# Chunk-selected attention and an ELU MLP on one NeuronCore: half-batch blocks in an order that the kernel's own list scheduler writes

## The chip, the cores and the metric

The kernel runs on one core of one Trainium2 chip. The core has five engines with a queue each, and every queue is worked off strictly in order: PE (TensorE: matrix products and transposes), ACT (ScalarE), DVE (VectorE), POOL (GpSimd) and SP (SyncE, which here only issues transfers). Engines wait for each other through semaphores. Products land in PSUM, which has eight banks of 512 float32 columns by 128 partitions. The metric is the device time of one execution in microseconds (us).

## The reference, cut to what matters

Four batches, eight heads, 768 positions, head width 64, all float32. Keys are cut into 24 chunks of 32. For each query and chunk an upper bound of the score is formed from the chunk's smallest and largest key values; each query keeps the six best causal chunks; softmax attention runs over those; the result, as 3072 tokens by 512, goes through a two-layer MLP with ELU between.

```python
ub = np.sum(np.maximum(q[:, :, :, None, :] * k_min[:, :, None, :, :], q[:, :, :, None, :] * k_max[:, :, None, :, :]), axis=-1)
causal = pos[:, None] // chunk >= np.arange(nc)[None, :]
ub = np.where(causal, ub, -1000000000.0)
top_chunks = np.argsort(ub, axis=-1)[..., -top_k:]
scores = scale * np.matmul(q, k.transpose(0, 1, 3, 2))
...
mask = sel & (pos[:, None] >= pos[None, :])
scores = np.where(mask, scores, -1000000000.0)
scores = scores - np.max(scores, axis=-1, keepdims=True)
attn = np.exp(scores)
attn = attn / (np.sum(attn, axis=-1, keepdims=True) + 1e-09)
return np.matmul(attn, v).astype(np.float32)
...
h = x @ w_in                      # 3072 x 512 @ 512 x 2048
g = np.where(h > 0.0, h, alpha * (np.exp(np.minimum(h, 0.0)) - 1.0))
return (g @ w_out).astype(np.float32)
```

## The kernel before

Heads go in pairs, 16 pairs in all, two pairs to a group. For each pair there are three stages, and for each half batch of 384 tokens there is the MLP.

- `prep` (L162): K and Q of the pair, all 768 positions, are transposed on PE in float32, three 128x128 transposes to a PSUM tile (`psK` L169, `psQ` L189). DVE takes the smallest and largest value of each chunk from the K tile (L172, L173); ACT copies the same tile as bf16 into `lhsA` and `lhsB` (L175, L176); POOL lays minimum and range into `kst` (L180, L181). ACT copies the Q tile to float32 (`QTf`) and twice to bf16 (`rhsA`, `rhsB`), and DVE clips `QTf` at zero (`Qrl`, L197). POOL casts V (`cast_v`, L118).
- `select` (L200): for a group of two pairs PE forms the bounds `ub` (L207), DVE transposes them (L210), finds the eight largest per query block (`MAX8`, L215), compares (L217) and transposes back (L221); SP sends the mask into the free rows of `rhsA` and `rhsB` (L224, L225), so that the score product adds it by itself.
- `attend` (L233): scores on PE (L250), exponential on ACT (L253, L256), the causal triangle on DVE (L262, L268), products with V on PE (L280, called PV here), normalising on DVE (L284, L286), transposing back on PE (L291) and copying to `xt` on DVE (L292).
- `mlp` (L295): sixteen first products of four matmuls (L302); each is followed by the exponential on ACT (L306), minus one on POOL (L308) and the join on DVE (L310) into `gT`; then three output tiles of sixteen matmuls (L315).

PSUM is dealt out in fixed shares: two banks for transposes and bounds, two for scores, one for PV, three for the MLP (L69 to L72). The program text runs groups in the order of L345 to L359: attention of two groups makes a batch, and the MLP of that batch is written two groups later, the last MLP at the end. The tile framework reorders the instructions of each engine by itself around that text. The weights are loaded by POOL, each load behind the cast of pair 2 to 5 (L327).

Two rules of the framework matter here. An instruction that reads or overwrites a tile waits for the instruction that last wrote or read it on another engine. And two engines that read the same PSUM bank are kept apart too, in the order in which the program gives the instructions.

Of the kernel before, what the change touches and what calls it, by code (L numbers as in the profile page):

```python
# [15 lines left out]
B = 4  # L16
H = 8
# [9 lines left out]
NQT = S // P  # L27
# [4 lines left out]
BIG = 3.0e38  # L32

NPAIR = H // 2
NSET = 4
Q0 = TOPK * CHUNK
NQB = NCH - TOPK
NQS = S - Q0
HB = NQB // 2
HQ = HB * CHUNK  # L40


@with_exitstack
def kernel(
# [29 lines left out]
    npairs = B * NPAIR  # L74


    def load(t):
        b, r = divmod(t, NPAIR)
        k_pair = ldpool.tile([P, NQT, 2, D], F32, name="k_pair")
        q_pair = ldpool.tile([P, NQT, 2, D], F32, name="q_pair")  # L80
        for h in range(2):
            nc.sync.dma_start(out=k_pair[:, :, h, :],
                              in_=k[b, 2 * r + h].rearrange("(n p) d -> p n d", p=P))
        for h in range(2):
            nc.sync.dma_start(out=q_pair[:, :, h, :],
                              in_=q[b, 2 * r + h].rearrange("(n p) d -> p n d", p=P))
        return k_pair, q_pair

    def load_v(t):
        b, r = divmod(t, NPAIR)  # L90
        v_pair = ldpool.tile([P, NQT, 2, D], F32, name="v_pair")
        for h in range(2):
            nc.sync.dma_start(out=v_pair[:, :, h, :],
                              in_=v[b, 2 * r + h].rearrange("(n p) d -> p n d", p=P))
        return v_pair

    lds = {t: load(t) for t in range(2)}
    ldv = {t: load_v(t) for t in range(2)}


    ident_f = const.tile([P, P], F32, name="ident_f")
    nc.gpsimd.memset(ident_f, 0.0)
    nc.gpsimd.affine_select(out=ident_f, in_=ident_f, compare_op=AOT.not_equal,
                            fill=1.0, base=0, pattern=[[-1, P]], channel_multiplier=1)
    ident_b = const.tile([P, P], BF16, name="ident_b")
    nc.vector.tensor_copy(out=ident_b, in_=ident_f)

    vexts, lhsA, lhsB, rhsA, rhsB, kst = [], [], [], [], [], []
    for s in range(NSET):
        vexts.append(const.tile([P, NQT, 2, D + 1], BF16, name=f"vext{s}"))  # L110
        lhsA.append(const.tile([P, S], BF16, name=f"lhsA{s}"))
        lhsB.append(const.tile([P, S], BF16, name=f"lhsB{s}"))
        rhsA.append(const.tile([P, S], BF16, name=f"rhsA{s}"))
        rhsB.append(const.tile([P, S], BF16, name=f"rhsB{s}"))
        kst.append(const.tile([P, 2, 64], F32, name=f"kst{s}"))

    def cast_v(t):
        return nc.gpsimd.tensor_scalar(out=vexts[t % NSET][:, :, :, 0:D], in0=ldv.pop(t), scalar1=1.0,  # L118
                                       scalar2=0.0, op0=AOT.mult, op1=AOT.add)

    for s in range(NSET):
        nc.vector.memset(kst[s], 0.0)
        nc.vector.memset(vexts[s][:, :, :, D:D + 1], 1.0)
        nc.vector.memset(rhsA[s][64:P, :], 0.0)
        nc.vector.memset(rhsB[s][0:64, :], 0.0)

    econst = const.tile([P, NCH, CHUNK], BF16, name="econst")
    nc.vector.memset(econst, MASKNEG)
    for r0 in (0, 64):
        nc.gpsimd.affine_select(out=econst[r0:r0 + 64], in_=econst[r0:r0 + 64],  # L130
                                compare_op=AOT.is_equal, fill=0.0, base=0,
                                pattern=[[1, NCH], [0, CHUNK]], channel_multiplier=-1)
    for s in range(NSET):
        nc.vector.tensor_copy(out=lhsA[s][64:P, :],
                              in_=econst[64:P].rearrange("p c w -> p (c w)"))
        nc.vector.tensor_copy(out=lhsB[s][0:64, :],
                              in_=econst[0:64].rearrange("p c w -> p (c w)"))

    tri01 = const.tile([P, P], BF16, name="tri01")
    nc.gpsimd.memset(tri01, 1.0)  # L140
    nc.gpsimd.affine_select(out=tri01, in_=tri01, compare_op=AOT.is_ge,
                            fill=0.0, base=0, pattern=[[1, P]], channel_multiplier=-1)
    selb = [const.tile([P, NQB, CHUNK], BF16, name=f"selb{i}") for i in range(2)]
    for i in range(2):
        nc.gpsimd.memset(selb[i], 0.0)

    w_in_sb = const.tile([P, NKK, DFF], BF16, name="w_in_sb")
# [200 lines left out]
    for g in range(ng):  # L348
        attend(2 * g)
        if g + 1 < ng:  # L350
            select(g + 1)
# [38 lines left out]
```

## Time and profile before

| | us |
|---|---|
| three runs, median (lowest to highest) | 381.0 (379.08 to 381.08) |
| the profiled execution, first to last instruction (its span) | 378.3 |
| PE busy | 318.7 |
| ACT busy | 225.4 |
| DVE busy | 205.3 |
| POOL busy | 103.3 |

The median of the runs is 2.7 us above the span of the profiled execution. Busy time counts each matmul from its start to its modelled end, and neighbours overlap, so the PE figure is no measure of how fast PE works; the rows below give starts as well. In the rows of the timeline a start in us comes first, then the duration, the engine, the source line, the operation, `output<-input`, the shape and a count; brackets at the end give the idle time before and who ended it.

### The profile page before, as it was taken

How to read it: one execution, taken by the hardware profiler on the slowest of the kernel's cores; microseconds unless marked ns; L12 is line 12 of the kernel's file. 1: busy time of each engine (PE TensorE's matmuls, PEld its weight loads, DVE VectorE, ACT ScalarE, POOL GpSimd, SP SyncE). 2: the span in 40 equal slices, each digit the busy share in tenths (PEclk: the TensorE clock that was granted, in tenths of full speed). 3: DMA queues.
4: the chain of work that ended last, by engine and by line, in shares of the span. 5: the costliest groups of instructions: out<-in, count | busy, mean ns of one | idle time of the engine just before them, and what ended most of it. 6: DMA issues, size and time to landing. Idle time of an engine off the chain costs nothing.

```text
span 378.3 us, 6504 instructions
## 1 busy us (share of the span) xinstructions
PE 318.7 (84%) x2260; PEld 176.6 (47%) x2272; DVE 205.3 (54%) x594; ACT 225.4 (60%) x489; POOL 103.3 (27%) x228
## 2 busy tenths in 40 slices
PE   1476876889599999599997799999999989979886
PEld 1333444455265455354564454545556444444442
DVE  7553275367477475561694683651867154261540
ACT  1638757858968965950879758653797052350430
POOL 4414022003133112340331231430123053250430
PEclk9995697589989999989998999999999999999999
DMA  9949999935914526501000000102000100101002
GB/s 205 277 74 192 203 181 177 280 71 118 209 42 98 125 71 161 117 2 55 30 12 2 1 14 28 58 0 83 5 11 2 57 29 26 58 3 55 28 2 83
DMA packets 84129, 30.67 MB, mean 81 GB/s; under 512 B 76160, under 2 KB 81024, under 8 KB 84096
## 3 DMA queue, kind: packets, MB, share of 16 engines
q1 hardware_dynamic: 79872, 26.06, 27.7%
q0 software_dynamic: 4224, 4.19, 7.1%
q8 instruction: 18, 0.29, 0.3%
q14 instruction: 15, 0.12, 0.1%
HBM read 27.26 MB, written 6.29 MB: 89 GB/s over the span
## 4 chain that ended last, share of the span: by engine, by line
PE 27%; issue 23%; ACT 21%; POOL 12%; DVE 11%; DMA 4%; POOLq 0%; SPq 0%; ACTq 0%; DVEq 0%
POOL m_sb L308 12%; PE o_ps L315 8%; ACT pt L253 6%; PE sps L250 4%; PE ub L207 4%; PE h_ps L302 4%; DMA k_pair<-in_k_dram 2%; DVE gT L310 2%; PE psQ L189 2%; ACT e_sb L306 2%; ACT QTf L194 1%; PE psK L169 1%; DMA rhsA_137<-selT 1%; ACT pt L256 1%; PE pxt L291 1%
## 5 line engine op out<-in xcount | busy, mean ns | idle before, releaser
L302 PE MATMUL h_ps<-xt,w_in_sb 128*128 128x384 bf16 x512 | 108.4, 333 | 13.2 <-DVE gT L310 12.8
L308 POOL TENSOR_SCALAR m_sb<-e_sb 128x384 f32<-128x384 f32 x128 | 65.9, 518 | 179.0 <-ACT e_sb L306 162.3
L253 ACT ACTIVATE pt<-sps 128x384 bf16<-128x384 f32 (+1 forms) x160 | 80.1, 536 | 37.2 <-PE sps L250 35.9
L310 DVE SCALAR_TENSOR_TENSOR gT<-h_ps,m_sb 128x384 bf16<-128x384 f32 x128 | 70.0, 554 | 43.7 <-POOL m_sb L308 40.4
L315 PE MATMUL o_ps<-w_out_sb,gT 128*128 128x512 bf16 x372 | 87.4, 379 | 0.6
L306 ACT ACTIVATE e_sb<-h_ps 128x384 f32<-128x384 f32 x128 | 62.3, 495 | 39.1 <-PE h_ps L302 37.8
L302 PEld LDWEIGHTS <-w_in_sb 128*128 128x128 bf16 x512 | 49.1, 99 | 49.1 <-issue 22.7
L315 PEld LDWEIGHTS <-gT 128*128 128x128 bf16 x384 | 36.9, 98 | 40.1 <-issue 1.0
L321 DVE COPY o_sb<-o_ps 128x512 f32<-128x512 f32 x16 | 11.0, 690 | 50.8 <-PE o_ps L315 50.8
L280 PEld LDWEIGHTS <-pt 128*128 128x128 bf16 x672 | 29.3, 102 | 16.4 <-DVE pt L262 6.4
L189 PE MATMUL psQ<-ident_f,q_pair 128*128 128x128 f32 x96 | 21.6, 345 | 17.8 <-ACT lhsB_124 L176 7.9
L319 ACT ACTIVATE o_sb<-o_ps 128x512 f32<-128x512 f32 x8 | 4.8, 597 | 39.5 <-PE o_ps L315 39.4
L169 PE MATMUL psK<-ident_f,k_pair 128*128 128x128 f32 x96 | 19.6, 323 | 8.7 <-DMA k_pair<-in_k_dram 4.3
L189 PEld LDWEIGHTS psQ<-ident_f,q_pair 128*128 128x128 f32 x96 | 12.4, 168 | 29.3 <-ACT lhsB_124 L176 10.5
L262 DVE TENSOR_TENSOR pt<-pt,tri_174 128x512 bf16<-128x512 bf16 x32 | 14.3, 446 | 12.8 <-ACT pt L253 12.6
L256 ACT ACTIVATE pt<-sps 128x512 bf16<-128x512 f32 x32 | 19.6, 611 | 1.4 <-PE sps L250 1.3
L197 DVE TENSOR_SCALAR Qrl<-QTf 128x576 f32<-128x576 f32 x16 | 7.4, 462 | 23.8 <-ACT QTf L194 23.8
L172 DVE TENSOR_REDUCE kmm<-psK 128x12 f32<-128x384 f32 x32 | 17.7, 552 | 4.2 <-PE psK L169 3.5
L169 PEld LDWEIGHTS psK<-ident_f,k_pair 128*128 128x128 f32 x96 | 11.9, 160 | 17.3 <-ACT rhsB_126 L196 5.3
L173 DVE TENSOR_REDUCE kmm<-psK 128x12 f32<-128x384 f32 x32 | 17.4, 545 | 0.0
L292 DVE COPY xt<-pxt 128x384 bf16<-128x384 bf16 x32 | 11.3, 353 | 11.2 <-PE pxt L291 10.7
L250 PE MATMUL sps<-rhsA_125,lhsA_123 128*128 128x384 bf16 (+2 forms) x36 | 10.3, 325 | 4.4 <-ACT pt L253 4.2
(220 smaller groups left out, 404.2 us busy)
## 6 DMA issues: line engine op xcount, KB each, us to landing
k_pair<-in_k_dram SPq DMA_DIRECT2D x32, 192.0 KB
q_pair<-in_q_dram SPq DMA_DIRECT2D x32, 192.0 KB
v_pair<-in_v_dram SPq DMA_DIRECT2D x32, 192.0 KB
out_dram<-o_sb SPq DMA_DIRECT2D x24, 256.0 KB
w_in_sb<-in_moe_w_in_dram POOLq DMA_DIRECT2D x4, 512.0 KB, 7.0
w_out_sb<-in_moe_w_out_dram POOLq DMA_DIRECT2D x4, 512.0 KB, 8.0
rhsA_125<-selT SPq DMA_DIRECT2D x4, 27.0 KB
rhsB_126<-selT SPq DMA_DIRECT2D x4, 27.0 KB
```

The lines of the kernel that those rows point to most:

```text
L169: nc.tensor.transpose(ps[:, P * n:P * (n + 1)], k_pair[:, 3 * h + n], ident_f)
L172: nc.vector.tensor_reduce(out=kmm[:, 0, cs], in_=pv, axis=AX.X, op=AOT.min)
L189: nc.tensor.transpose(ps[:, P * n:P * (n + 1)], q_pair[:, 3 * h + n], ident_f)
L250: nc.tensor.matmul(sps[:, o + pc:o + pc + w], lhsT=lhs[hd][:, P * kb:P * (kb + 1)], rhs=rhs[hd][:, c0:c0 + w], start=True, stop=True)
L253: nc.scalar.activation(out=pt[:, hd, 0:wtot], in_=sps[:, 0:wtot], func=AF.Exp, scale=SCALE)
L256: nc.scalar.activation(out=pt[:, :, 0:256], in_=sps[:, :].rearrange("p (h w) -> p h w", h=2), func=AF.Exp, scale=SCALE)
L280: nc.tensor.matmul(o3[:, hd, qi, :], lhsT=pt[:, hd, P * qt + off:P * qt + off + P], rhs=vexts[s][:, kb, hd, :], start=(kb == 0), stop=(kb ...
L302: nc.tensor.matmul(hw, lhsT=w_in_sb[:, kk, P * fc:P * (fc + 1)], rhs=xT[NPAIR * b + kk][:, ts], start=(kk == 0), stop=(kk == NKK - 1))
L306: nc.scalar.activation(out=e_sb, in_=hw, func=AF.Exp)
L308: nc.gpsimd.tensor_scalar(out=m_sb, in0=e_sb, scalar1=-1.0, scalar2=1.0, op0=AOT.add, op1=AOT.mult)
L310: nc.vector.scalar_tensor_tensor(out=gT[:, fc, :], in0=hw, scalar=0.0, in1=m_sb, op0=AOT.max, op1=AOT.min)
L315: nc.tensor.matmul(o_ps, lhsT=gT[:, fc, P * tt:P * (tt + 1)], rhs=w_out_sb[:, fc, :], start=(fc == 0), stop=(fc == NFC - 1))
```

## The change

The unit of work becomes the half batch: for each of eight blocks (batch b, half h of 384 positions) `prep` transposes half of K and Q of each of the four pairs, `select` covers the queries of that half (192 of them in the first half, 384 in the second), `attend` runs the half, and the MLP of the block follows. The arithmetic, the matmul shapes of scores, PV and MLP and the total of transposes are as before. K, V and the minimum and maximum of the first half stay for the second.

All operations are entered into a graph with the engines that may run them and an estimated duration, and a list scheduler in the kernel (`Graph.run`) plays them through: at each point an engine takes the operation of lowest priority number that is ready and for which a buffer is free. What comes out is each engine's order, each operation's buffer, and for copies out of PSUM whether ACT or DVE does them. The instructions are issued in that order with the framework's own reordering off (`manual_schedule`). Priorities come from a few numbers that place attention blocks and MLP blocks on one axis; loads stand 14 units and preparations 7 units ahead of their block. The eight PSUM banks form one pool for all stages. All constants are set up before the first scheduled operation, now for eight `lhsA`/`lhsB` pairs (four on DVE, four on POOL) and twenty half-width `rhs` tiles. Loads move half a batch each, so there are 192 instead of 96, and 64 mask transfers instead of 32. The scheduler's graph knows that a reader waits for the writer; it has no entry for two engines that read the same bank.

```diff
-    psT = pool("psT", 2, space=bass.MemoryType.PSUM)
-    psS = pool("psS", 2, space=bass.MemoryType.PSUM)
-    psO = pool("psO", 1, space=bass.MemoryType.PSUM)
-    psM = pool("psM", 3, space=bass.MemoryType.PSUM)
...
+    slots("bank", 8, [P, 512], F32, psum)
+    slots("kf", 6, [P, 3, 2, D], F32)
...
+    slots("e", 3, [P, HS], F32)
+    slots("m", 3, [P, HS], F32)
+    slots("gT", 26, [P, HS], BF16)
...
+        for b, key in reads:
+            if key in b.last_w:
+                o.deps.add(b.last_w[key])
+            b.readers.setdefault(key, []).append(o)
+        for b, key in writes:
+            if key in b.last_w:
+                o.deps.add(b.last_w[key])
+            for r in b.readers.get(key, ()):
+                if r is not o:
+                    o.deps.add(r)
...
+                    while i < len(lst):
+                        o = lst[i][2]
...
+                        for b in o.bufs:
+                            if b.slot is None and not any(ft <= t for ft, _ in free[b.cls]):
+                                ok = False
+                                break
+                        if ok:
+                            pick = o
+                            lst.pop(i)
+                            break
...
+def c_act(n):
+    return {ACT: (n / 1.2 + 66, n / 1.2 + 175)}
+
+
+def c_dve(n, psum=True):
+    return {DVE: (n / 0.96 + 70, n / 0.96 + (160 if psum else 100))}
...
+        for t in store["kst"]:
+            nc.vector.memset(t, 0.0)
+        for i in range(8):
+            eng = nc.vector if i < 4 else nc.gpsimd
+            for t, r in ((store["lhsA"][i], slice(64, P)), (store["lhsB"][i], slice(0, 64))):
+                eng.tensor_copy(out=t[r, :], in_=econst[r].rearrange("p c w -> p (c w)"))
+        for h in range(2):
+            for t in store[f"rhsA{h}"]:
+                nc.vector.memset(t[64:P, :], 0.0)
...
+    W_GATE = [2, 3, 4, 5, 6, 7, 8, 9]
...
+        g.op("kmin" + tag, c_dve(HS), red(0, AOT.min), reads=[(bank, 0)], writes=[(kmm, 0)], prio=prio)
+        g.op("kmax" + tag, c_dve(HS), red(1, AOT.max), reads=[(bank, 0)], writes=[(kmm, 1)], prio=prio)
...
+        evac(prio + 0.5, la, lo, ts, bank, name="ka")
+        evac(prio + 0.5, lb, hi, ts, bank, name="kb")
...
-    for g in range(ng):
-        attend(2 * g)
-        if g + 1 < ng:
-            select(g + 1)
...
+    for i in range(2 * B):
+        b, h = divmod(i, 2)
+        w = att_at[i + 1] - att_at[i]
+        for gr in range(2):
+            for r in (2 * gr, 2 * gr + 1):
+                prep(b, h, r, att_prio(i, 0.25 * r) - PREPAHEAD)
+            select(b, h, gr, att_prio(i, 0.5 * gr) - PREPAHEAD + 2.0)
+        for r in range(NPAIR):
+            attend(b, h, r, att_prio(i, 0.25 * r), 0.25 * w)
...
+    order = g.run()
...
+    with tc.manual_schedule():
+        consts()
+        for o in order:
+            o.emit(o.engine)
```

What the scheduler makes of it is seen in the order on the engines. First DVE at the program's start, before; `kmm` are the chunk minima and maxima, `lhsA` and `lhsB` the K copies whose free rows take the constant `econst`:

```order
L106 CAST ident_b<-ident_f 128x128
L128 MEMSET econst 128x768
L172 TENSOR_REDUCE kmm<-psK 128x12
L173 TENSOR_REDUCE kmm<-psK 128x12
L136 COPY lhsB_124<-econst 64x768
L136 COPY lhsB_130<-econst 64x768
L134 COPY lhsA_123<-econst 64x768
```

DVE at the same place now; `bank_61` and `bank_63` hold transposed K, `bank_62` transposed Q, and in front of these rows stand the eight copies of `econst` and eighteen more memsets like the first two:

```order
L304 MEMSET rhsB_129 64x192
L304 MEMSET rhsB_130 64x192
L392 TENSOR_REDUCE kmm_139<-bank_61 128x12 x2
L406 CAST rhsA_111<-bank_62 64x384
L443 TENSOR_SCALAR qr_146<-qt_142 128x192
L392 TENSOR_REDUCE kmm_140<-bank_63 128x12 x2
L406 CAST rhsA_112<-bank_64 64x384
```

The first minima stood ahead of the copies of constants and stand now behind all of them and behind twenty memsets; DVE also has copies out of PSUM (`rhsA` from `bank_62`) that ACT had.

Next ACT, with the semaphores that each row waits for, the second K tile of pair 0 and the first of pair 1, before; `psK` is the transposed K:

```order
L175 ACTIVATE lhsA0_123<-psK_201 64x384 [waits DVE_49]
L176 ACTIVATE lhsB0_124<-psK_201 64x384
L196 ACTIVATE rhsB0_126<-psQ_215 64x384
L194 ACTIVATE QTf_213<-psQ_222 128x384 [waits PE_49]
L195 ACTIVATE rhsA0_125<-psQ_222 64x384
L196 ACTIVATE rhsB0_126<-psQ_222 64x384
L175 ACTIVATE lhsA1_129<-psK_241 64x384 [waits DVE_49,PE_49]
```

ACT now, pairs 0 and 1 of the first block; `bank0` and `bank2` hold K, `bank1` and `bank3` hold Q:

```order
L404 ACTIVATE lhsA0_87<-bank0_61 64x384 [waits PE_49]
L404 ACTIVATE lhsB0_95<-bank0_61 64x384 [waits DVE_49]
L438 ACTIVATE qt0_142<-bank1_62 128x192 [waits PE_49]
L404 ACTIVATE rhsB00_116<-bank1_62 64x384 [waits DVE_49]
L404 ACTIVATE lhsA1_88<-bank2_63 64x384 [waits PE_49]
L404 ACTIVATE lhsB1_96<-bank2_63 64x384 [waits DVE_49]
```

Before, ACT waited once for a K tile, until both reductions on DVE had read it. Now the first copy goes ahead of the minimum, and the second copy waits for DVE, which has read the same bank in between; 13 of the 32 K banks are read in this way, ACT and DVE by turns (copy, minimum, copy, maximum), and four more in the opposite turn.

Last PE among attention and MLP, in the third group before; `h_ps` is a tile of the MLP's first product, `o3` the PV product, `sps` the scores:

```order
L280 MATMUL o3_2781<-vext2_134,pt_2758 128x65
L302 LDWEIGHTS w_in_sb_181
L302 MATMUL h_ps_3166<-xt_1159,w_in_sb_181 128x384
L302 LDWEIGHTS w_in_sb_181
L302 MATMUL h_ps_3166<-xt_1315,w_in_sb_181 128x384
L302 LDWEIGHTS w_in_sb_181
L302 MATMUL h_ps_3166<-xt_1527,w_in_sb_181 128x384
L189 MATMUL psQ_2696<-ident_f_115,q_pair_1848 128x128 x3
```

PE now, where the MLP of the first block gives way to the scores of the second; `xt0` to `xt3` are the four pairs' results:

```order
L626 MATMUL bank1_62<-xt1_175,w_in_sb_228 128x384
L626 LDWEIGHTS w_in_sb_228
L626 MATMUL bank1_62<-xt2_176,w_in_sb_228 128x384
L626 LDWEIGHTS w_in_sb_228
L626 MATMUL bank1_62<-xt3_177,w_in_sb_228 128x384
L530 LDWEIGHTS lhsA0_87
L530 MATMUL bank2_63<-rhsA10_121,lhsA0_87 128x384
L530 LDWEIGHTS lhsB0_95
L530 MATMUL bank6_67<-rhsB10_126,lhsB0_95 128x384
```

The MLP's matmuls, single ones between attention work before, now come in fours to a bank, and the first six of these groups go to six different banks, where three were to be had.

## Rows read from the trace of the kernel before

**Rows 1.** The page's part on engines: busy us, share of the span, instructions.

```profile
PE 318.7 (84%) x2260; PEld 176.6 (47%) x2272; DVE 205.3 (54%) x594; ACT 225.4 (60%) x489; POOL 103.3 (27%) x228
```

**Rows 2.** Windows: from:to, length, each engine's busy us, PEclk, DMA share, GB/s.

```profile
0.00:80.00 80.00, 52.05 (x328) 30.32 (x330) 40.76 (x134) 47.95 (x101) 21.48 (x51) 0.79 0.99 196
80.00:301.00 221.00, 201.08 (x1597) 113.39 (x1603) 132.96 (x405) 152.11 (x337) 57.26 (x129) 0.98 0.21 56
```

**Rows 3.** Timeline of PE: the pace of each kind of matmul, by neighbouring starts.

```profile
49.73 0.41 PE L207 MATMUL ub<-QTf,kst_139 128*64 128x288 f32 x1
...
49.97 0.41 PE L207 MATMUL ub<-Qrl,kst_139 128*64 128x288 f32 x1
...
118.54 0.50 PE L169 MATMUL psK<-ident_f,k_pair 128*128 128x128 f32 x3
118.87 0.23 PE L280 MATMUL o_1544<-vext_134,pt 128*128 128x65 bf16 x2
...
283.60 0.85 PE L280 MATMUL o_3845<-vext_134,pt 128*128 128x65 bf16 x22
284.29 0.32 PE L250 MATMUL sps<-rhsA_143,lhsA_141 128*128 128x384 bf16 x1
...
288.85 1.46 PE L302 MATMUL h_ps<-xt,w_in_sb 128*128 128x384 bf16 x8
290.17 0.38 PE L315 MATMUL o_ps<-w_out_sb,gT 128*128 128x512 bf16 x1
...
364.07 10.52 PE L315 MATMUL o_ps<-w_out_sb,gT 128*128 128x512 bf16 x47
```

**Rows 4.** Windows of 280 to 300, PE alone, lines L302, L315, L250, L280 in turn.

```profile
280.00:300.00 20.00, 6.28 (x27) 1.00 0.04 15
280.00:300.00 20.00, 8.60 (x39) 1.00 0.04 15
280.00:300.00 20.00, 5.13 (x24) 1.00 0.04 15
280.00:300.00 20.00, 3.42 (x72) 1.00 0.04 15
```

**Rows 5.** Timeline at the end: the last three MLP halves begin; the last copy.

```profile
301.86 2.11 PE L302 MATMUL h_ps<-xt,w_in_sb 128*128 128x384 bf16 x12
...
304.50 2.11 PE L302 MATMUL h_ps<-xt,w_in_sb 128*128 128x384 bf16 x12 [0.53 <-DVE gT L310]
...
374.63 0.69 DVE L321 COPY o_sb<-o_ps 128x512 f32<-128x512 f32 x1 [6.21 <-PE o_ps L315]
```

**Rows 6.** Timeline of the start: constants on DVE and POOL, the first minimum.

```profile
1.26 0.38 DVE L124 MEMSET rhsA_125<- 64x384 uint32 x1
...
5.91 0.70 DVE L128 MEMSET econst<- 128x768 bf16 x1
...
6.53 0.49 DVE L172 TENSOR_REDUCE kmm<-psK 128x12 f32<-128x384 f32 x1
6.68 2.23 POOL L130 TENSOR_SCALAR_AFFINE_SELECT econst<-econst 64x768 bf16<-64x768 bf16 x2 [3.90 <-DVE econst L128]
...
7.98 1.14 DVE L136 COPY lhsB_130<-econst 64x768 bf16<-64x768 bf16 x1
...
9.41 0.35 DVE L134 COPY lhsA_129<-econst 64x768 bf16<-64x768 bf16 x1
...
```

**Rows 7.** Groups of DVE by line: count, busy us and mean ns, idle before.

```profile
L172 DVE TENSOR_REDUCE kmm<-psK 128x12 f32<-128x384 f32 x32 | 17.7, 552 | 4.2 <-PE psK L169 3.5
L292 DVE COPY xt<-pxt 128x384 bf16<-128x384 bf16 x32 | 11.3, 353 | 11.2 <-PE pxt L291 10.7
```

**Rows 8.** Timeline: a K tile read by DVE, then by ACT.

```profile
15.55 0.55 DVE L173 TENSOR_REDUCE kmm<-psK 128x12 f32<-128x384 f32 x1
16.20 0.48 ACT L175 ACTIVATE lhsA_129<-psK 64x384 bf16<-64x384 f32 x1 [0.77 <-DVE kmm L173]
```

**Rows 9.** The page's part on transfers: KB each, us from issue to landing.

```profile
w_out_sb<-in_moe_w_out_dram POOLq DMA_DIRECT2D x4, 512.0 KB, 8.0
```

More of the change, by code (lines that the diff above doesn't have):

```diff
@@ L1 @@
+import bisect
+import heapq
 from contextlib import ExitStack
@@ L26 @@
 P = 128
-NQT = S // P
 HS = S // 2
@@ L34, with __init__ @@
 NPAIR = H // 2
-NSET = 4
 Q0 = TOPK * CHUNK
[L37 to L40, printed above, removed]
+PE, ACT, DVE, POOL, SP = "PE", "ACT", "DVE", "POOL", "SP"
+SEM = 45.0
+class Buf:
+    __slots__ = ("cls", "left", "slot", "end", "last_w", "readers")
+    def __init__(self, cls):
+        self.cls = cls
+        self.left = 0
+        self.slot = None
+        self.end = 0.0
+        self.last_w = {}
+        self.readers = {}
+class Op:
+    __slots__ = ("name", "engines", "emit", "deps", "nexts", "bufs", "prio", "seq", "wait",
+                 "ready", "start", "finish", "engine", "xfer", "gate")
@@ L43, with c_both, c_pool, c_mm @@
+def c_act(n):
+    return {ACT: (n / 1.2 + 66, n / 1.2 + 175)}
+def c_dve(n, psum=True):
+    return {DVE: (n / 0.96 + 70, n / 0.96 + (160 if psum else 100))}
+def c_both(n):
+    return {**c_act(n), **c_dve(n)}
+def c_pool(n):
+    return {POOL: (n * 1.03 + 60, n * 1.03 + 110)}
+def c_mm(widths):
+    t = sum(w / 2.4 + 2.5 for w in widths)
+    return {PE: (t, t + 170)}
+def c_dma(e=SP, issue=420.0):
+    return {e: (issue, issue)}
 @with_exitstack
@@ L89, in load_v @@
[L89 to L98, printed above, removed]
+    const = ctx.enter_context(tc.tile_pool(name="const", bufs=1))
+    psum = ctx.enter_context(tc.tile_pool(name="psum", bufs=1, space=bass.MemoryType.PSUM))
@@ L108 @@
[L108 to L125, printed above, removed]
-    econst = const.tile([P, NCH, CHUNK], BF16, name="econst")
[L128 to L142, printed above, removed]
@@ L200, in select @@
-    def select(g):
-        ubT = selpool.tile([P, NQB, CHUNK], F32, name="ubT")
-        for u in range(2):
-            ub = psT.tile([P, HQ], F32, name="ub", tag="ps")
+        g.op(f"w_out{i}", c_dma(POOL, 900.0),
+             lambda e: nc.gpsimd.dma_start(out=w_out_sb[:, 4 * i:4 * i + 4, :],
+                                           in_=wo[:, 4 * i:4 * i + 4, :]),
+             writes=[(fixed, ("wo", i))], prio=-1.0, xfer=3400.0, after=[casts[W_GATE[4 + i]]])
+    ATT_W = [10.0, 19.0]
+    att_at = [0.0]
@@ new lines, with att_prio, mlp_prio, dma @@
+    for i in range(8):
+        att_at.append(att_at[-1] + ATT_W[i % 2])
+    W_GATE = [2, 3, 4, 5, 6, 7, 8, 9]
+    casts = []
+    def att_prio(i, frac):
+        return att_at[i] + frac * (att_at[i + 1] - att_at[i])
+    MLP0, MLPW = 14.0, 15.1
+    def mlp_prio(i, frac):
+        return MLP0 + MLPW * (i + frac)
+    LOADAHEAD = 14.0
+    PREPAHEAD = 7.0
+    lhs = {}
+    rhs = {}
+    vx = {}
+    qq = {}
+    ks = {}
+    xT = {}
+    def dma(dst_src, writes, reads, prio, xfer, name):
+        def emit(e):
+            d, s_ = dst_src()
+            nc.sync.dma_start(out=d, in_=s_)
+        g.op(name, c_dma(), emit, reads=reads, writes=writes, prio=prio, xfer=xfer)
@@ L363 @@
+    order = g.run()
+    kernel.graph = (g, order)
+    with tc.manual_schedule():
+        consts()
+        for o in order:
+            o.emit(o.engine)
 _INS = ['q', 'k', 'v', 'moe_w_in', 'moe_w_out']
```

616 lines of the change are left out of this document (424 added, 192 removed).

## The prediction

> **What bounds the kernel now.** I read the page's part on engines first, then windows along the span, then the timeline of PE for the pace of each kind of matmul. PE is busy 318.7 us of 378.3, ACT 225.4, DVE 205.3, POOL 103.3 [rows 1]. The reader should not take the 84% at its word: a matmul's row runs to its modelled end and overlaps the next one, so I count work by starts. From [rows 3]: eight matmuls of the MLP's first product take 1.32 us from the first start to the next instruction's, 0.165 each (0.43 ns a column); its second product 10.52 for a tile set of 48, 0.219 each; PV 22 in 0.69, 0.031 each; three float32 transposes 0.33; one step of the bounds (288 columns, both pairs side by side) 0.24. All work at that pace:
>
> - MLP: 512 x 0.165 = 84.5 and 384 x 0.219 = 84.1
> - scores: 86,016 columns x 0.43 ns = 37.0
> - PV: 672 x 0.031 = 21.1
> - 64 sets of three transposes x 0.33 = 21.1
> - bounds: 16 x 4 steps x 0.24 = 15.4
> - transposing the results: 96 x 128 columns x 0.43 ns = 5.3
>
> That is 268.5 us: PE does 71% of what it could in 378.3, and 110 us are to be had from it alone. Where they lie: up to 80 us PE is busy 52.05 us at a granted clock of 0.79 of full speed, 41 us of work at most [rows 2]. From 301.86 to the last copy at 374.63 run three whole MLP halves, 192 x 0.165 + 144 x 0.219 = 63.2 us in 72.8, 87%; three groups share three banks and PE then waits 0.53 for DVE [rows 5]. So the middle, 222 us, holds at least 268.5 - 41 - 63.2 = 164 us, 74%. In a stretch of it where attention and MLP mix well, 280 to 300, the counts give 27 x 0.165 + 39 x 0.219 + 24 of 288 scores (3.1) + 72 x 0.031 = 18.4 of 20, 92% [rows 4]. The bound is PE, fed badly: late at the start, by few banks later.
>
> The Trainium skill (Perfetto Trace Analysis, Identifying the Most-Contended Engine) says that matmul busy share is not a good measure of how near TensorE is to its limit. Here 84% stands against 71% by starts; by the busy share the change could win at most 60 us.
>
> **The change, part by part.** *Work.* Columns of every kind are as before, so 268.5 us stay. ACT and DVE keep their operations too; copies only move between them (25 out of PSUM from ACT to DVE by the order, 12 of the MLP's output copies the other way). With 225 and 205 us of busy time neither bounds a kernel of 330 us by itself.
>
> *The start*, up to the first MLP matmul. DVE is what PE waits for: minima, bounds and normalising are all on it, in order. First constants, which the graph does not count: `econst` 0.70, then POOL's two selects on it, 2.23, so DVE can copy from about 4 us; eight copies at 0.35 and twenty memsets of half the width of one that took 0.38, about 0.22 each: 4 + 2.8 + 4.4 = 11 us, where the first minimum stood at 6.53 before [rows 6]. But one such copy took 1.14 while POOL's select ran, and now POOL makes eight copies of that shape at the same time; the select, the nearest row, took 1.1 for one. If each DVE copy waits for one on POOL, 8 x 1.45 instead of 2.8: 20 us. I take 14, nearer the 11, because one of eight copies in the trace was held up.
>
> The skill's page SBUF — State Buffer (Who interferes with whom) says that VectorE's fast copies and GpSimd share a port pair that is locked for a whole instruction, and that the second to issue blocks fully. The row of 1.14 agrees; by the rule the start is the 20 us, and everything 6 us later.
>
> Then DVE has 71 scheduled operations ahead of its first MLP join, with durations between 0.353 and 0.552 [rows 7]; at 0.45 that is 32 us (25 to 39). Last the hand-overs on banks: a K tile is now often read copy, minimum, copy, maximum, with ACT and DVE by turns, and each waits for the other. From [rows 8] ACT starts 0.10 after DVE's end, so such a tile takes 2 x 0.48 + 2 x 0.55 + 3 x 0.1 = 2.4 us, of which DVE stands still about 0.7; a Q tile shared with DVE adds some. Nine preparations come before the first join; I take 0.9 each, 8 us (0, where DVE has other work in between, to 12). Sum: 14 + 32 + 8 = 54 us; ends 36 and 71, of which I keep 45 to 62 for the range.
>
> *Transfers in the start.* The first mask stands behind 34 half-size loads on SP, 3.3 MB, some 17 us at the 196 GB/s of the first 80 us [rows 2]; DVE has it ready at about 24 us, so they cost nothing. POOL issues the weights behind casts and pieces of `kst`, the last two of the second matrix behind its sixth MLP operation, at about 58 us; landing takes 8.0 [rows 9], so they are there at 68, when PE is still in the first MLP product and the scores between. Nothing is charged; if they were late, PE would wait some 5 us once.
>
> *After the start.* Up to the first MLP matmul PE has done 19 sets of transposes (6.3), bounds for 1152 columns (3.8), scores of 6144 (2.6), 48 PV (1.5) and 12 result transposes (0.7): 14.9 us. 253.6 are left. How full PE runs then decides. The nearest rows: 74% at least in the middle of before, where preparation mixes in, and 92% where it does not. For the upper end: eight banks instead of three take the 0.53 waits away, a group of MLP matmuls stands ready beside every attention step in PE's order, and the load of the others is under 70%. Against it: every hand-over on a K bank stands at the head of two queues, and the graph does not know of it, so the orders were made for tiles that free a bank a microsecond earlier. I take 90%: 253.6 / 0.90 = 282 us.
>
> *The end.* Nothing but PE's own work in the last block; from the last tile's copy to the end of the span 3.7 us as before (374.63 to 378.3) [rows 5].
>
> Sum: 54 + 282 + 3.7 = 340 us of span against 378.3. The runs lie 2.7 us above the span at the median, so **342 us**, 10% below 381.
>
> **Rivals.**
>
> 1. PE is fed almost without a gap. For it: the 92% were reached with three banks, and the other engines have slack everywhere. Against it: DVE and ACT hand banks to each other 32 times more than planned. With a start of 48 and 96%: 48 + 264 + 6.4 = 318 us.
> 2. The hand-overs cost PE in every preparation and the fill stays as it was. For it: before, with none of these turns, PE reached 74 to 80% wherever preparations ran. Against it: PE has MLP groups in between. At 80%: 54 + 317 + 6.4 = 377 us, between a little faster and the same.
> 3. Slower: the same mechanism uncovered. The queues are strict, so an ACT copy that waits for a minimum holds the exponentials behind it, and PE's score and PV matmuls behind those; each of 32 K banks then costs PE its full 2.4 us: with 95% otherwise 54 + 267 + 77 + 6.4 = 404 us. It decides from (381 - 54 - 267 - 6.4) / 32 = 1.7 us lost on PE for each K bank, or, said otherwise, from a fill of 79% down.
> 4. The change does not do what it says for the start, because the constants on two engines collide (20 us) and the sum comes to its upper end, 71: 71 + 282 + 6.4 = 359 us.
>
> **How the numbers follow.** Forecast 342, with starts of 45 to 62 and fills of 86 to 95%: 45 + 267 + 6.4 = 318 to 62 + 295 + 6.4 = 363. Chances: forecast 0.66, rival 1 0.13, rival 4 0.08, rival 2 0.08, rival 3 0.05. The range 318 to 363 holds the forecast, rival 4 and half of rival 1. Faster by over 0.5% (about what a measurement of this kernel tells from no change) takes in the forecast, rivals 1 and 4 and most of rival 2: 0.92; the same 0.03; slower 0.05.
>
> **What would show it.** PE's first MLP matmul between 45 and 62 us, with DVE busy from about 14 us to there almost without a gap. After it, PE's work by starts at 86 to 95% of each window and the granted clock near full. The last two MLP halves without the wait for the join on DVE. In the waits, ACT's second K copy waiting for the minimum, and DVE's maximum for ACT, each under a microsecond; if PE's scores or PV then wait for ACT or DVE some 1.7 us per K bank, rival 3 is right. The forecast fails if PE is still under 80% filled between 100 and 250 us, or if the first MLP matmul comes after 70.

## The result, and the profile after

| | before | after |
|---|---|---|
| median of the runs (lowest to highest), us | 381.04 (379.08 to 383.05) | 331.62 (329.64 to 331.95) |
| span of the profiled execution, us | 378.3 | 330.2 |
| time of that execution above its span, us | 2.7 (median) | 1.75 |

The ratio is 0.869, 95% interval 0.865 to 0.873: 13% faster. The forecast was 342, with 318 to 363 as its range.

The page's part on engines, after, beside [rows 1]:

```profile
PE 290.7 (88%) x2272; PEld 172.8 (52%) x2272; DVE 215.5 (65%) x652; ACT 213.8 (65%) x477; POOL 125.1 (38%) x324
```

The busy share of PE moved by four points only; counted by starts with the paces of [rows 3], PE did 71% of what it could before, and does 81% now (268.5 of 330.2). This share of work by starts is called the fill below. Where the time came from is read by the same count over stretches of the span. Up to 82 us PE did 28.6 us of work before and 34.9 now; from 82 to 300 us 172.9 (79%) before and 207.3 (95%) now. The trace of before lacks 12 records of the second product in that stretch, 2.6 us of work; with them it is 81%, and at 300 us some 38 us less is left to do now. The other 10 of the 48.1 us that the span lost are the end: from 300 us to its last matmul PE was filled to some 86% before, and is full now. Windows of after (from:to, length, busy us of PE, PEld, DVE, ACT, POOL with counts, granted clock, DMA share, GB/s), beside [rows 2]:

```profile
14.00:54.00 40.00, 24.42 (x157) 15.10 (x158) 28.03 (x91) 22.06 (x48) 16.06 (x48) 0.91 0.84 154
54.00:82.00 28.00, 22.65 (x181) 13.36 (x181) 16.16 (x47) 16.56 (x38) 13.99 (x30) 0.94 0.84 163
82.00:150.00 68.00, 66.40 (x550) 39.93 (x547) 48.48 (x149) 49.30 (x112) 26.97 (x70) 1.00 0.52 126
150.00:225.00 75.00, 73.45 (x620) 44.70 (x619) 51.16 (x159) 58.59 (x136) 26.16 (x74) 1.00 0.29 74
225.00:300.00 75.00, 73.69 (x620) 44.14 (x619) 50.74 (x155) 54.11 (x122) 22.64 (x59) 1.00 0.09 28
```

In the last three lines PE hardly waits (3.4 us of 218 in all); the first two are where time is left: transfers at 0.84 of what the engines can, none of DVE, ACT and POOL busy for more than 70%. PE's fill is 72% from 54 to 82, then 94, 95 and 97%.

The start, from the timeline (start, duration, engine, line): constants on DVE and POOL side by side, the first minimum, the first turns on a K bank, the first MLP matmul, beside [rows 6, 8]:

```profile
4.38 0.35 DVE L299 COPY lhsB<-econst 64x768 bf16<-64x768 bf16 x1
4.74 0.89 DVE L299 COPY lhsA<-econst 64x768 bf16<-64x768 bf16 x1
5.64 0.88 DVE L299 COPY lhsB<-econst 64x768 bf16<-64x768 bf16 x1
...
13.56 1.05 DVE L304 MEMSET rhsB<- 64x192 uint32 x5
14.54 0.48 DVE L392 TENSOR_REDUCE kmm<-bank 128x12 f32<-128x384 f32 x1
```

```profile
4.58 0.84 POOL L299 COPY lhsA<-econst 64x768 bf16<-64x768 bf16 x1
5.46 0.86 POOL L299 COPY lhsB<-econst 64x768 bf16<-64x768 bf16 x1
```

```profile
15.05 0.48 ACT L404 ACTIVATE lhsB<-bank 64x384 bf16<-64x384 f32 x1 [9.58 <-DVE kmm L392]
```

```profile
54.34 4.18 PE L626 MATMUL bank<-xt,w_in_sb 128*128 128x384 bf16 x24
```

From 4.58 on DVE's copies come every 0.90 us, where the one before took 0.35: the collision of rival 4 is real. Its price was 3.2 us (six copies, 0.54 each), not the 9 between my 11 and 20, so the first minimum stands at 14.54 (forecast 14) and the first MLP matmul at 54.34 (forecast 54).

The one large hole after that, on four engines:

```profile
72.23 0.51 POOL L451 TENSOR_SCALAR vext<-vf 128x384 bf16<-128x384 f32 x1 [4.83 <-DMA vf<-in_v_dram]
72.70 2.88 POOL L638 TENSOR_SCALAR m<-e 128x384 f32<-128x384 f32 x6
73.25 1.91 ACT L634 ACTIVATE e<-bank 128x384 f32<-128x384 f32 x4 [4.91 <-POOL m L638]
73.25 1.03 DVE L642 SCALAR_TENSOR_TENSOR gT<-bank,m 128x384 bf16<-128x384 f32 x2 [5.25 <-POOL m L638]
75.34 0.34 PE L609 MATMUL bank<-ident_b,on 128*128 128x128 bf16 x3 [4.29 <-DVE on L598]
```

Read it from the top: a cast of V at the head of POOL's queue waits 4.83 us for its load; six MLP operations stand behind it; ACT and DVE stand behind those; PE behind DVE. The chain of waits leads back to the same transfers:

```profile
47.88 5.80 DMA kf<-in_k_dram
...
63.71 8.37 DMA vf<-in_v_dram
```

Groups by line (busy us, mean ns, idle before): the first MLP product, beside the same line of the profile of before with 13.2 us of idle time ahead of it, 12.8 of it for the join on DVE; and from the waits the hand-overs on K banks (us in total, times, longest):

```profile
L626 PE MATMUL bank<-xt,w_in_sb 128*128 128x384 bf16 x512 | 94.8, 329 | 0.4 <-ACT pt L542 0.3
```

```profile
ACT lhsB L404 <- DVE kmm L392: 18.3, 16, 9.6
DVE kmm L392 <- ACT lhsA L404: 9.4, 16, 1.0
DVE kmm L392 <- ACT lhsB L404: 4.3, 9, 0.6
```

Leave out the 9.58 of the start, and a turn (one engine waiting until the other has read the bank) costs ACT 0.6 and DVE 0.55 us, of which next to nothing reaches PE after 82 us. The end, beside [rows 5]:

```profile
306.43 9.91 PE L626 MATMUL bank<-xt,w_in_sb 128*128 128x384 bf16 x60
316.18 10.52 PE L653 MATMUL bank<-w_out_sb,gT 128*128 128x512 bf16 x48
```

```profile
326.74 0.60 ACT L661 ACTIVATE o<-bank 128x512 f32<-128x512 f32 x1 [2.86 <-PE bank L653]
```

One MLP half is left for the end instead of three.

### The profile page after: what moved, and what is told of

It reads as the page before. It is cut to its first block, busy times and chain, and to the rows that moved or that the text cites. A ratio compares the mean times of both kernels' runs of the same rounds, so it can differ in the third digit from the quotient of the medians.

```text
span 330.2 us, 6933 instructions
## 1 busy us (share of the span) xinstructions
PE 290.7 (88%) x2272; PEld 172.8 (52%) x2272; DVE 215.5 (65%) x652; ACT 213.8 (65%) x477; POOL 125.1 (38%) x324
## 4 chain that ended last, share of the span: by engine, by line
PE 59%; DVE 16%; ACT 12%; DMA 5%; issue 4%; POOL 2%; SPq 1%; DVEq 0%; ACTq 0%; POOLq 0%
PE bank L653 23%; PE bank L626 16%; PE bank L530 6%; PE bank L383 5%; PE bank L584 4%; ACT pt L542 4%; PE bank L468 4%; DVE kmm L392 3%; DMA vf<-in_v_dram 3%; DVE gT L642 2%; DMA kf<-in_k_dram 2%; PE bank L609 2%; ACT e L634 2%; ACT lhsA L404 1%; ACT rhsA L404 1%
## 5 line engine op out<-in xcount | busy, mean ns | idle before, releaser
L626 PE MATMUL bank<-xt,w_in_sb 128*128 128x384 bf16 x512 | 94.8, 329 | 0.4 <-ACT pt L542 0.3
L638 POOL TENSOR_SCALAR m<-e 128x384 f32<-128x384 f32 x128 | 64.8, 517 | 79.7 <-ACT e L634 70.6
L653 PE MATMUL bank<-w_out_sb,gT 128*128 128x512 bf16 x384 | 93.9, 382 | 0.1
L542 ACT ACTIVATE pt<-bank 128x384 bf16<-128x384 f32 (+1 forms) x160 | 75.2, 577 | 12.4 <-PE bank L530 12.3
L642 DVE SCALAR_TENSOR_TENSOR gT<-bank,m 128x384 bf16<-128x384 f32 x128 | 67.3, 546 | 23.9 <-POOL m L638 22.2
L634 ACT ACTIVATE e<-bank 128x384 f32<-128x384 f32 x128 | 61.7, 516 | 22.1 <-PE bank L626 12.0
L392 DVE TENSOR_REDUCE kmm<-bank 128x12 f32<-128x384 f32 x64 | 34.6, 551 | 14.6 <-ACT lhsA L404 9.4
L530 PE MATMUL bank<-rhsB,lhsB 128*128 128x384 bf16 x144 | 36.0, 294 | 2.0 <-DVE gT L642 0.8
L530 PE MATMUL bank<-rhsA,lhsA 128*128 128x384 bf16 x144 | 36.6, 296 | 0.9 <-DVE gT L642 0.3
L661 ACT ACTIVATE o<-bank 128x512 f32<-128x512 f32 x20 | 11.9, 596 | 28.6 <-PE bank L653 28.5
L584 PE MATMUL bank<-vext,pt 128*128 128x65 bf16 x672 | 26.9, 194 | 2.1 <-DVE pt L565 1.3
L557 DVE TENSOR_TENSOR pt<-pt,tri 128x512 bf16<-128x512 bf16 x32 | 13.8, 432 | 17.9 <-ACT pt L542 17.9
```

The source lines that it names most:

```text
L392: nc.vector.tensor_reduce(out=ap(kmm)[:, w, :], in_=ap(bank)[:, 0:HS].rearrange("p (c w) -> p c w", w=CHUNK), axis=AX.X, op=op)
L530: nc.tensor.matmul(ap(banks[hd])[:, o + pc:o + pc + wd], lhsT=ap(ls[hd])[:, P * kb:P * (kb + 1)], rhs=ap(rs[hd])[:, c0 - HS * h:c0 - HS * ...
L542: lambda e, hd=hd, pt=pt, banks=banks, wtot=wtot: nc.scalar.activation(out=ap(pt)[:, hd, 0:wtot], in_=ap(banks[hd])[:, 0:wtot], func=AF.Ex ...
L584: nc.tensor.matmul(o3v()[:, hd, qi, :], lhsT=ap(pt)[:, hd, P * qi + off:P * qi + off + P], rhs=ap(vx[b, r])[:, kb, hd, :], start=(kb == 0) ...
L626: nc.tensor.matmul(ap(bank)[:, 0:HS], lhsT=w_in_sb[:, kk, P * fc:P * (fc + 1)], rhs=ap(xT[b, h, kk]), start=(kk == 0), stop=(kk == NKK - 1))
L634: lambda e, eb=eb, bank=bank: nc.scalar.activation(out=ap(eb), in_=ap(bank)[:, 0:HS], func=AF.Exp),
```

## The experiments

Ratios are to the kernel before, timed beside each run. Three landmarks are read from each trace: the first matmul of the MLP's first product, the first of its second product, and the start of the last 60 first products.

| run | median, us | ratio to before, 95% | first product | second product | last 60 |
|---|---|---|---|---|---|
| the changed kernel | 331.6 | 0.865 to 0.873 | 54.34 | 77.78 | 306.43 |
| fixed_shares | 343.7 | 0.899 to 0.907 | 60.05 | 81.80 | 314.87 |
| mlp_after_batch | 362.0 | 0.947 to 0.955 | 93.57 | 103.97 | 334.31 |
| framework_order | 328.1 | 0.860 to 0.867 | 56.47 | 76.19 | 302.51 |
| known_turns | 325.5 | 0.852 to 0.861 | 53.49 | 71.79 | 300.03 |
| planner_nudge | 332.0 | 0.869 to 0.876 | 58.75 | 77.00 | 306.33 |
| quarter_weights | 325.1 | 0.850 to 0.857 | 53.35 | 71.37 | 299.36 |
| late_constants | 326.9 | 0.855 to 0.862 | 55.44 | 73.87 | 301.89 |
| vf_8 | 337.2 | 0.881 to 0.888 | 57.55 | 75.68 | 311.07 |
| spread_constants | 325.9 | 0.855 to 0.862 | 52.91 | 70.93 | 300.41 |
| spread_turns | 321.8 | 0.843 to 0.850 | 50.16 | 68.31 | 294.77 |
| spread_order | 331.6 | 0.870 to 0.877 | 57.43 | 78.00 | 304.22 |
| spread_turns_order | 334.7 | 0.877 to 0.885 | 57.03 | 83.77 | 309.53 |

All runs but fixed_shares and mlp_after_batch have done the same 31.0 us of work on PE when the second product starts. From there to the last 60 all of these but vf_8 (235 us) take 226 to 230 us, so what such a variant gains or loses it has done by then. The first product says less: planner_nudge has it 4.4 us late and loses nothing.

**What the middle gained.** fixed_shares goes back to shares of the banks:

```diff
-    slots("bank", 8, [P, 512], F32, psum)
+    slots("psT", 2, [P, 512], F32, psum)
+    slots("psS", 2, [P, 512], F32, psum)
+    slots("psO", 1, [P, 512], F32, psum)
+    slots("psM", 3, [P, 512], F32, psum)
...
-        bank = g.buf("bank")
+        bank = g.buf("psT")
...
```

> The changed kernel with PSUM dealt out again as before: two banks for transposes and bounds, two for scores, one for PV, three for the MLP; the scheduler plans with these shares, everything else as changed. Theory (the shared pool of eight banks is what lifts PE's fill behind the start from about 80 to 95%): 345 to 365 us, PE's work by starts between 82 us and 300 us under 90%, and waits of PE for the join on DVE again in the last two MLP halves. Rival (the order and the half batches carry the gain, the pool only makes planning easy): 329 to 336 us, fill within 2 points of 95%.

343.7, 12 us slower than the changed kernel: just under the range of the theory, far from the rival. PE waits again for the join (2.6 us of it after 300 us), and its K transposes for the reductions (groups by line, as above):

```profile
L629 PE MATMUL psM<-xt,w_in_sb 128*128 128x384 bf16 x512 | 98.7, 329 | 4.9 <-DVE gT L645 4.4
...
L386 PE MATMUL psT<-ident_f,kf 128*128 128x128 f32 x96 | 19.2, 316 | 19.2 <-DVE kmm L395 13.8 <-POOL tri L293 4.2 <-ACT rhsB L407 1.3
```

By starts PE did 195.1 us of work from 82 to 300 where the changed kernel did 207.3 (18 records of its second product are missing here, 3.9 us), a fill of 89 to 91%, at the edge of the theory's 90. Up to 82 us it did as much in both (35.2 and 34.9), although the 13.8 us of K transposes waiting for reductions lie there. So eight to twelve us are lost in the middle and nothing before it; PE's waits from 82 to 300 come to 9.0 us, against 3.4 in the changed kernel.

mlp_after_batch keeps everything but lets an MLP block start only after its whole batch is attended to:

```diff
+        last_xt[b, h] = g.op("xt" + tag, {DVE: (275, 360)},
...
-                 writes=[(bank, 0)], prio=pr)
+                 writes=[(bank, 0)], prio=pr, after=[last_xt[b, 1]])
```

> The changed kernel, but the MLP of a batch's first half may only start when the attention of its second half is done, as whole-batch work has it; blocks, banks and scheduler stay. Theory (the early MLP fills PE while attention is bound by ACT and DVE): the first MLP matmul moves from 54 to 75 to 85 us and the time to 339 to 348 us, since of the 20 to 30 us only some 16 us of attention work for PE can be done meanwhile. Rival (the MLP is made up for later at no loss): under 335 us.

362.0, 30 us slower: the direction of the theory at about twice its size. The first MLP matmul came at 93.57, not at 75 to 85, and PE without MLP beside attention runs slowly and at a lower granted clock:

```profile
54.00:82.00 28.00, 19.59 (x147) 12.01 (x148) 16.65 (x65) 17.93 (x42) 9.56 (x30) 0.74 0.88 170
82.00:150.00 68.00, 61.47 (x458) 35.26 (x462) 34.96 (x102) 41.29 (x88) 24.07 (x53) 0.96 0.46 113
```

At its second product (103.97) PE had done 43.3 us of work, 12.3 more than the changed kernel at 77.78; from there to the last 60 its fill is 88% (17 missing records counted), against 95. From these figures I estimate that some 13 of the 30 us are lost before that point and some 16 behind it.

So of the parts taken out one at a time the half-batch MLP as filler is the largest, and the common banks are the second. The half batches without the kernel's own scheduler were not run. framework_order takes the planner's order only as a list:

```diff
-    with tc.manual_schedule():
-        consts()
-        for o in order:
-            o.emit(o.engine)
+    consts()
+    for o in order:
+        o.emit(o.engine)
```

> The changed kernel with its blocks, buffers and choice of engines, but the instructions are handed to the tile framework without manual order, so that the framework sorts each engine's queue by itself again. Theory (the scheduler's order is worth much): 340 to 370 us. Rival (half batches and the shared banks carry the gain, and any reasonable order does): within 1% of 331.6 us. A third outcome, that the framework leaves the given order nearly alone, would show as equal orders on PE.

328.1, 3.5 us faster by the medians, with ranges that just touch (327.9 to 330.2 against 329.6 to 332.0): the theory that the strict order is worth time fell here. But the third outcome is near as well. By tile name 2098 of PE's 2272 weight loads start in the same place of its order, so the framework keeps most of what the planner wrote, and the run doesn't show what a kernel without the planner's list would take. What the order does is seen below.

**What holds the start.** known_turns tells the planner that the K copies come after both reductions:

```diff
+        reds = [
+            g.op("kmin" + tag, c_dve(HS), red(0, AOT.min), reads=[(bank, 0)], writes=[(kmm, 0)], prio=prio),
+            g.op("kmax" + tag, c_dve(HS), red(1, AOT.max), reads=[(bank, 0)], writes=[(kmm, 1)], prio=prio)]
...
-        evac(prio + 0.5, la, lo, ts, bank, name="ka")
-        evac(prio + 0.5, lb, hi, ts, bank, name="kb")
+        evac(prio + 0.5, la, lo, ts, bank, name="ka", after=reds)
+        evac(prio + 0.5, lb, hi, ts, bank, name="kb", after=reds)
```

> The changed kernel with one edge more in the graph: the two copies of a K bank by ACT (or DVE) wait for both reductions by DVE, as in the kernel before; so no K bank is read by turns, and the scheduler knows it. Theory (the hand-overs of banks stand on ACT and DVE and cost PE nothing behind the start): 327 to 335 us; ACT's waits for DVE at the second K copy fall from 18 us to under 5, and the first MLP matmul moves by less than 4 us. Rival (each hand-over reaches PE, 1 us or more for each of 17 banks): 310 to 322 us.

325.5, 6 us faster, between the two. The first MLP matmul moved by less than 1 us, as the theory has it; ACT's wait for DVE at its K copies fell to 15.7 us, 9.4 of it at the start, and not under 5. The middle is as before; all of the gain stands at the second product already (71.79 against 77.78). Whether an order is lucky was asked by planner_nudge:

```diff
-    def run(self, dma_lat=(700.0, 1300.0)):
+    def run(self, dma_lat=(700.0, 1330.0)):
```

> One assumed latency of a load in the planner goes from 1300 to 1330 ns. Nothing that the chip does is changed except the order in which the planner lists the same instructions. It measures how far the time moves with the order alone. Theory (the orders are all about as full): within 1.5 us of 331.6. Rival (the order of the changed kernel has one costly hole by chance, at 71 to 75 us, and others miss it): 325 to 329, by which the 6 us that known_turns gained would be mostly this chance and not its edit.

332.0, within 0.4 us, although 160 of PE's 2272 weight loads (by tile name) stand in another place of its order and the wait of 4.29 is not in its trace. The rival fell for this one order: filling that hole alone gains nothing, since the work before it comes later. quarter_weights leaves every order and leaves out three quarters of the weight loads; the MLP reads the loaded quarter four times over:

```diff
-            out=w_in_sb[:, :, 512 * i:512 * (i + 1)], in_=wi[:, :, 512 * i:512 * (i + 1)]
+            out=w_in_sb[:, 0:1, 512 * i:512 * (i + 1)], in_=wi[:, 0:1, 512 * i:512 * (i + 1)]
-            out=w_out_sb[:, 4 * i:4 * i + 4, :], in_=wo[:, 4 * i:4 * i + 4, :]
+            out=w_out_sb[:, 4 * i:4 * i + 1, :], in_=wo[:, 4 * i:4 * i + 1, :]
...
-            lhsT=w_in_sb[:, kk, P * fc:P * (fc + 1)]
+            lhsT=w_in_sb[:, 0, P * fc:P * (fc + 1)]
...
-            rhs=w_out_sb[:, fc, :]
+            rhs=w_out_sb[:, 4 * c, :]
```

> The eight weight loads fetch one quarter of their bytes (1 MB in place of 4 MB), and the MLP's matmuls read the loaded quarter four times over; the order of instructions on every engine stays that of the changed kernel, and so do all matmuls' shapes. The output is not the reference's. Theory (the loads share of 0.8 to 1.0 between 30 and 80 us is what makes the V load of 63.71 late, holds POOL's queue at the V cast for 4.83 us and leaves TensorE idle for 4.3 us at 71 to 75): that wait falls under 1 us and the kernel gains 4 to 9 us, 322.5 to 327.5. Rival (the stretch is paced by VectorE and the hand-overs, transfers late by chance only): within 1.5 us of the changed kernel's 331.6, 330 to 333, and TensorE stands idle there for another reason. Both say that the first MLP matmul, at 54.34, moves by less than 2 us.

325.1, 6.5 us faster, and the wait is gone: the theory. With the same instructions in the same order, 3 MB less to fetch is worth 6.5 us: transfers are among what bounds the stretch up to 78 us. late_constants moves constants behind the first transposes (ten memsets of the second half, and the copies for pairs 4 to 7):

```diff
+            if o.name == "kT010":
+                rhs_consts((1,))
+            if o.name == "kT100":
+                lhs_consts(range(4, 8), nc.gpsimd)
```

> The copies of the mask rows into the tiles of pairs 4 to 7 (eight on POOL) and the eighty... second-half zeroes on VectorE are issued after the first key transposes rather than before them; nothing is left out. Theory (the start is a sum on VectorE, so what stands before the first minimum at 14.54 us is paid in full): the first minimum comes at 10 to 12 us, the first MLP matmul at 50 to 52, the kernel at 327 to 330. Rival (from 30 us on the loads pace the start, so an earlier minimum waits for them): the first MLP matmul stays within 1 us of 54.34 and the time within 1 us of 331.6.

326.9, at the lower end of the theory's range, but not by its path: the first minimum came at 9.95, 4.6 us sooner, and the first MLP matmul at 55.44, later than before. On POOL and PE:

```profile
45.75 0.82 POOL L282 COPY lhsA<-econst 64x768 bf16<-64x768 bf16 x1
...
51.81 0.82 POOL L282 COPY lhsB<-econst 64x768 bf16<-64x768 bf16 x1
...
52.95 1.54 PE L473 MATMUL bank<-qr,kst 128*64 128x384 f32 x2 [5.26 <-POOL kst L427]
```

The eight copies in a row held a piece of `kst` for 7 us. What gained is in the transfers: tenths of the DMA engines' busy time, 8 to 88 us in steps of two, of the changed kernel, known_turns, late_constants and spread_turns in turn:

```profile
DMA  8788870000399999999989999486999958812678
```

```profile
DMA  8788772008999999998999957567999965138878
```

```profile
DMA  8878880039999999999999668685999991777884
```

```profile
DMA  8887881999999999999994884899999505888760
```

In the changed kernel the loads stand still from 20 to 28 us. The order of SP's queue, its wait, and PE's K transposes of the second pair tell why:

```profile
17.78 1.03 SPq L352 DMA_DIRECT2D qf<-in_q_dram  x2
24.77 0.89 SPq L352 DMA_DIRECT2D rhsA<-selT  x1
...
27.99 1.05 SPq L352 DMA_DIRECT2D vf<-in_v_dram  x2
```

```profile
SPq L352 <- DVE selT L499: 5.9, 1, 5.9
```

```profile
5.95 0.87 PE L383 MATMUL bank<-ident_f,kf 128*128 128x128 f32 x3 [0.27 <-DMA kf<-in_k_dram]
```

Behind 34 loads the first mask stands at the head of the queue, and SP waits 5.9 us until DVE has written it (`selT`, at 24.74); the next loads go out behind the mask's four transfers, at 27.99. Full tiles do not explain it: five of V's six tiles were in use, and PE had read the first two K tiles by 6.82. In framework_order, with the same tiles, two loads of V and one of K go ahead of the mask, from 18.85 on. From 30 us the loads run at the limit to about 72, but for a dip at 58 to 64.

The mask comes from the minima, so an earlier first minimum or quicker turns send it sooner: at 22.68 in known_turns, 20.20 in late_constants and 18.91 in spread_turns. The four empty steps become two, two and none; the loads behind the mask start again 2.1, 4.6 and 5.9 us sooner, and the second product comes 6.0, 3.9 and 9.5 us sooner: the same direction, not the same sizes, so the loads are not shown to be all of it. planner_nudge sends the mask at 24.80 and has the same four empty steps, and the same time. A run that moves only the mask in SP's queue was not made.

vf_8 gives V more tiles:

```diff
-    slots("vf", 6, [P, 3, 2, D], F32)
+    slots("vf", 8, [P, 3, 2, D], F32)
```

> Eight tiles for loaded V in place of six. Theory (a V load waits for a free tile, since SP's queue takes them in turn, and lands late at the cast): V is issued earlier, the wait of 4.83 us at the cast goes, and the time falls by 3 to 6 us, to 325.5 to 328.5. Rival (the transfers themselves are full between 30 and 70 us; V that is fetched earlier takes the place of K or Q): within 1.5 us of 331.6, with a longer wait of TensorE for K in its place.

337.2, 5.6 us slower, beyond both. The standstill stays, since the mask still goes out at 24.80; and later PE waits for masks (waits of PE from 82 to 225 us), which the changed kernel never does:

```profile
PE bank L530 <- DMA rhsA<-selT: 2.8, 1, 2.8
PE bank L530 <- DMA rhsB<-selT: 1.6, 3, 0.8
```

These 4.4 us come near the 5.6 lost. Whether the loads in SP's queue delay the masks was not tried, and the planner's whole order is another one here too, so that other orders can cost more than planner_nudge's 0.4 us is not ruled out.

**Putting it together.** spread_constants sends those eight copies to ACT, two ahead of each pair:

```diff
-            if o.name == "kT100":
-                lhs_consts(range(4, 8), nc.gpsimd)
+            if o.name in ("kT100", "kT101", "kT102", "kT103"):
+                lhs_consts([4 + int(o.name[-1])], nc.scalar)
```

> As late_constants, with nothing left out, but the eight copies of mask rows for pairs 4 to 7 go to ScalarE, two ahead of each pair of the next batch, in place of one run of eight on POOL, which in late_constants held a bounds product for 5.26 us at 47.7 to 52.95. Theory (the start is paid in full; late_constants gave its 4.6 us back in that run of copies): first minimum at 10 us as there, first MLP matmul at 48.5 to 51, time 320 to 325. Rival (the loads pace the stretch before 54 us): first MLP matmul within 1.5 us of late_constants' 55.44 or the changed kernel's 54.34, the loads' share over 0.95 from 30 us on, and the time within 1.5 us of late_constants' 326.9.

325.9: the rival's time. The first MLP matmul moved up to 52.91, just inside the rival's 1.5 us, and the loads are at their limit from 26 to 52 us.

spread_turns has this edit and that of known_turns:

> spread_constants and known_turns together. If the 6 us of known_turns come from the hand-overs before 54 us and are a sum with the start: 5 to 6 us under spread_constants. If both shorten the same stretch, in which the loads are full, they share one gain: within 2 us of the better of the two.

321.8, 4.1 us under spread_constants and 3.8 under known_turns: between one shared gain and a sum, and the best version run. It is 3% faster than the changed kernel and 15% faster than the one before.

The last two add the edit of framework_order, to spread_turns and to spread_constants:

> spread_turns, with the engines' order left to the framework from the planner's list, as in framework_order, which took 3.5 us off the changed kernel. Theory (that gain was the same hole at 71 to 75 us, which is gone here): within 1.5 us of spread_turns. Rival (the framework's order is fuller everywhere): 3 to 4 us under it.

> spread_constants with the engines' order left to the framework, without the planner's knowledge of the turns. Theory: within 1.5 us of spread_constants. Rival: 3 to 4 us under it. Beside spread_turns_order it shows what the turns are worth when the framework sets the order: nothing if it finds them by itself, 5 to 6 us if not.

334.7 and 331.6, 13 and 6 us slower than with the strict order, which none of the theories had. In spread_order POOL issues the weights from 8.77 us on, in spread_constants from 23.45, and PE's wait for K in spread_order is the last line:

```profile
8.77 0.98 POOL L322 DMA_DIRECT2D w_in_sb<-in_moe_w_in_dram  x1
```

```profile
23.45 0.98 POOL L322 DMA_DIRECT2D w_in_sb<-in_moe_w_in_dram  x1
```

```profile
PE bank L392 <- DMA kf<-in_k_dram: 20.4, 5, 7.6
```

The planner holds a weight load behind a cast in its graph alone; the framework sees no such dependency and pulls the loads forward. Ahead of the K loads that goes with 20.4 us of waiting on PE up to 54 us, where spread_constants has 1.0; spread_turns_order has its first weights at 8.76 and 18.0 us of this wait. In framework_order they came at 17.61, into the standstill, which fits its gain; that this is all of it was not tested.

## Why the prediction came out as it did

By its own terms, for the profiled execution: start 54 (measured 54.34); PE's work after it 253.6 (253.3); fill 90% (93.0%: 253.3 in the 272.4 us from 54.34 to 326.70), so 282 became 272.4; end 3.7 (3.5); between span and run 2.7 (1.75; later runs of the kernel before lie 1.7 above their own spans as well, so 1 us of the 2.7 was scatter between runs). The sum is 331.95 against 342: 9.6 of the 10 us are the fill.

- **Fill, mis-sized.** I took the 92% of [rows 4] as the upper neighbour and went below it for the hand-overs. From 82 us on it is 95%. fixed_shares and mlp_after_batch show what carries it: eight to twelve us of the middle hang on the common banks, and 30 of the whole on the MLP of half a batch that starts early and runs beside attention. Neither was priced by itself.
- **Hand-overs.** About 0.6 us each (the longest 1.0, the start aside), near the forecast, and hidden from PE after 82 us: rivals 2 and 3 are out. In the start they cost: with them known to the planner 6 us go, near the 8 I charged, but at the second product and not at the first, where I charged them (53.49 against 54.34).
- **The start: right in size, wrong in make-up.** DVE was to be busy from 14 to 54 almost without a gap; it was busy for 28 of 40 us. The constants' part is right to 0.5 us. But late_constants began 4.6 us sooner and had its first MLP matmul 1.1 us later, so the start is no sum on DVE, and 54 against 54.34 is in part luck.
- **Constants on two engines (rival 4).** The Trainium skill's page SBUF — State Buffer (Who interferes with whom) has the second engine wait for a whole instruction of the other; a DVE copy and a POOL copy in turn would then make a step of 0.35 + 0.85 = 1.2 us, by my estimate from the rows. The trace shows 0.90, with POOL's copies at 0.85 nearly as long as alone (0.82 in late_constants): DVE slows down to POOL's step, no more.
- **Transfers, charged nothing: the step that failed.** I added up 17 us of loads ahead of the first mask, found it ready at 24 us (24.74) and took that to cost nothing; I did not ask what stands behind the mask. All later loads of K, Q and V do: transfers stand still for 8 us and then take all that the DMA engines can move to about 72 us. quarter_weights prices 3 MB in that stretch at 6.5 us; the standstill has no price of its own. The 5 us for a late transfer that I named came, but for V on POOL and not for the weights. The loss stands in the fill (72% from 54 to 82), so without it the fill would have been further off the forecast still.
- **Rival 1** took 96%, as far above the 93.0% as the forecast's 90 is below it, and a start that was too short (48): 318.

## What to carry to other kernels

Price a mixed schedule by what each stage has beside it to fill PE: here work that is ready early is worth more than any single wait removed. When a start gets a new order, draw up the account of its transfers too: ask of each queue not only what stands ahead of a transfer but what stands behind it while it waits for its source. More tiles do not help loads that such a transfer holds, as vf_8 shows. A gate that only a planner knows holds only where the planner's order is kept.

## What the runs showed of the hardware that was not expected

- DVE's 64x768 bf16 copy takes 0.35 us alone and 0.88 while POOL makes the same copy, whose own 0.85 hardly changes (0.82 alone).
- From 54 to 82 us attention without MLP beside it had a mean granted clock of 0.74 of full speed (mlp_after_batch, PE busy 19.59 us of 28), that is about half of the time at each of the two levels, 2.4 and 1.2 GHz; with MLP beside it 0.94 (22.65 us).
